# Constant matmuls ahead of weight blocks, earlier value loads, a mask moved to TensorE, and paired reciprocals

## The chip, the cores and the metric

The kernel runs on one core of a Trainium2 chip. The metric is the device time of one execution in microseconds (us). TensorE does the matmuls and transposes, VectorE and ScalarE the element-wise work, GpSimd a share of the latter, and SyncE (SP) issues every transfer between memory and the core's buffer. Each engine works through its own instructions in the order in which they were written; semaphores tie the engines together.

## The reference, cut to what matters

Three layers in a row, all in fp32: attention with a causal mask and a bias from cumulated sums, a gated layer without an activation, and a layer with a squared ReLU.

```python
# q, k, v: (4, 8, 576, 64), s: (4, 8, 576); q and k are eight times 0.1 * randn
cum    = np.cumsum(np.maximum(s, 0.0), axis=-1)
bias   = -(cum[..., :, None] - cum[..., None, :])
scores = 0.125 * q @ k^T + np.minimum(bias, 0.0)      # -1e9 above the diagonal
attn   = softmax(scores);   x = (attn @ v), as (2304, 512)
x      = ((x @ w_a) * (x @ w_b)) @ w_out              # 512 -> 1536 -> 512
out    = np.maximum(x @ w_in, 0.0) ** 2 @ w_out2      # 512 -> 2048 -> 512
```

## The kernel before, in words

The order of all instructions is written by a planner (class `Plan`). The kernel first traces every operation with the engines that may run it, an estimated cost for each, and the buffers that it takes. `Plan.order` then simulates the engines with these costs: at each step it takes, for the engine that is free first, the most urgent operation that is ready. Urgency is the stream ("first", "next", "att", "moe", "late", "fill") and then the order of tracing. A transfer may be issued while no more than 3 us of planned transfers are outstanding; a buffer of a tag is handed out in the order of tracing. An operation may carry a `lag`, a time to add to its readiness. A changed cost or lag can thus change the order everywhere behind it.

`Plan.run` emits the instructions in that order. An operation on TensorE may carry a number `idle`: so many matmuls of a constant tile `warm` (128 x 512, bf16) are emitted just ahead of it, into the PSUM bank that the operation itself writes (`op.bank`). The planner sets `idle` by itself where it sees a gap of over 400 ns ahead of an operation, and takes the larger of that and a number that was set by hand; by hand it is set to 6 ahead of the first scores of heads 0 and 2. The constants take no time in the plan. They stop where the pools are swapped, after the attention.

Attention works on a batch at a time, two heads (a pair) at a time, the queries cut into blocks of 96 and four times 120 rows. `softmax` makes a head's scores in PSUM, in five diagonal pieces (the last block has one more, without the diagonal): in the first batch (`b == 0`) by fp32 matmuls of `fq` and `fk`, whose 65th row holds the cumulated sums; in the others by two fp32r matmuls of split operands. The causal mask has two forms, by the constant `MASKED`. For `b < MASKED` a further matmul adds a triangle of -1e9 (`mask`, bf16, times the identity `plain`) to the diagonal's columns, and VectorE reduces the scores to the negated maximum (`neg`). Otherwise one VectorE operation, recorded as CUSTOM_DVE_ANT_0 and followed by a read of its accumulator, adds the mask, negates the scores in PSUM and gives the minimum; the exponential then takes a scale of -1. ScalarE's exponential (`e<-st,neg`) leaves row sums in `tot`; VectorE adds them into `one` and takes the reciprocal of a head's five columns. `weigh` transposes the weights (`pt`), copies them (`ph`) and multiplies them with the values (`av`); `divide` multiplies the pair's result with the reciprocals of both heads.

The sums start the kernel: `ssb` is loaded, VectorE scans it into `cum`, and a row of `cum` per head is sent by a transfer to the 65th row of `fk`. The values of the very first pair carry a lag of `SUMS_FIRST` = 5800 ns. The tag of the value tiles has two buffers.

Then comes `moe1`, the gated layer, in chunks of 512 tokens. A block `fstep(f)`, f from 0 to 11, makes two half blocks in banks of the tag "mm", which has three buffers: `ab{c}_{f}_0` with `w_a` and `ab{c}_{f}_1` with `w_b`, twelve matmuls each. ScalarE copies the first to `a`, VectorE multiplies the second with it in its bank, ScalarE and VectorE then split the product from that bank into `gh` and `gl`. Three blocks are summed with `w_out` (`py`). Chunk 0 uses the first batch's tokens while the weights are still being decoded: `split_w(f)` loads the three pieces of 512 KB of a block, a few raw buffers at a time (`roomxh`, `roomxl`, `words`), and VectorE, ScalarE and GpSimd turn them into `wh` and `wl`. Interleaved with chunk 0 runs the attention of the second batch. Later chunks load what chunk 0 stored. The squared-ReLU layer follows after the swap.

All instructions of the program are recorded under line 261 (constants: 256), so tiles tell them apart.

Of the kernel before, what the change touches and what calls it, by code (L numbers as in the profile page):

```python
# [16 lines left out]
P = 128  # L17
# [246 lines left out]
def attention_moe_moe(tc, q, k, v, s, w_a, w_b, w_out, w_in2, w_out2, out):  # L264
# [28 lines left out]
    SOON = 2  # L293
    BEHIND = 2
    AHEAD = 5
    SUMS_FIRST = 5800.0
    LATE_DOWN = 7
    APART = 2
    READY = 6
# [1 line left out]
    pl = Plan(nc)  # L301
# [55 lines left out]
    def dve(*args, reads=(), **kw):  # L357
        pl.call(on_dve(*args, **kw), reads=reads)
# [53 lines left out]
    def load_values(b, p):  # L412

        t = at([P, NJ, P], F32, "val", 2, f"val{b}_{p}")
        j = 0
        while j < len(kb):
            k0, m = kb[j]
            j1 = j + 1
            while j1 < len(kb) and kb[j1][1] == m:
                j1 += 1  # L420
            dma(
                t[:m, j:j1].part(j),
                v[b, p, k0 : k0 + m * (j1 - j)].rearrange("(j t) c -> t j c", t=m), m * (j1 - j) * 0.5,
                lag=SUMS_FIRST if b == 0 and p == 0 else 0.0,
            )
            for i in range(j, j1):
                values[b, p, i] = t[:m, i].part(j)
            j = j1
# [66 lines left out]


    HALF = S // 2
    MASKED = 1
    banks = [[(2, 0, 336), (0, 0, 96)], [(1, 0, 216), (LAST, 0, HALF)], [(LAST, HALF, HALF)], [(3, 0, 456)]]
    places = {0: ("e0", 432, 0), 2: ("e0", 432, 96), 1: ("e1", 672, 0), 3: ("e1", 672, 216), LAST: ("e2", S, 0)}  # L500

# [84 lines left out]
    def softmax(b, p, h, head, one):  # L586

        nq = len(kb)
        nm = f"{b}_{p}_{h}"
        hh = 2 * p + h  # L590
        neg, tot = small[count[1] % 4]
        count[1] += 1
        tiles, place, held = {}, {}, []
        for blk, (tag, width, off) in places.items():
            if tag not in tiles:
                tiles[tag] = at([P, width], F32, tag, 3, f"{tag}{nm}")
            place[blk] = (tiles[tag], off)
        for i, pieces in enumerate(banks):
            ps = mm_bank(f"st{nm}_{i}") if b == 0 and i % 4 > 1 else bank(f"st{nm}_{i}")
            off = 0  # L600
            calls, cost, got = [], 0, []
            for blk, k0, kn in pieces:
                at_, m = kb[blk]
                qc = slice(at_, at_ + m)
                to = ps[:m, off : off + kn]
                diag = at_ >= k0 and at_ + m <= k0 + kn
                ks = slice(k0, k0 + kn)
                if b == 0:
                    tq, tk = head
                    both = ((tq[: D + 1, qc], tk[: D + 1, ks]),)  # L610
                    cost += 4 * kn / 2.4 + 13
                else:
                    t1, t2q, t2k = head
                    both = ((t1[:66, 0, qc], t1[:66, 1, ks]), (t2q[:, qc], t2k[:, ks]))
                    cost += 2 * (kn / 2.4 + 15)
                calls += [("matmul", (to, *ab), {"stop": True}) for ab in both]
                if diag and b < MASKED:
                    tri = mask[:m, EDGE : EDGE + m]
                    calls.append(("matmul", (to[:, kn - m :], plain[:m, :m], tri), {"stop": True}))
                    cost += 70  # L620
                e, eo = place[blk]
                got.append((blk, k0, m, to, kn, diag, e[:m, eo + k0 : eo + k0 + kn]))
                off += kn
            if b == 0:
                ins = [tq.part("x"), tq.part("c"), tk.part("x"), tk.part("c")]
            else:
                ins = [t1, t2q, t2k]
            if b < MASKED:
                ins += [plain, mask]

            for z, (_, _, kw) in enumerate(calls):
                kw.update(start=z == 0, skip_group_check=z > 0)
            pe(cost, calls, ps, ins)
            if b == 0 and i == 0 and hh in (0, 2):
                pl.ops[-1].idle = 6
            for blk, k0, m, to, kn, diag, _ in got:
                c = blk if k0 == 0 else nq
                if not diag or b < MASKED:
                    dve("tensor_reduce", kn, out=neg[:m, c : c + 1].part(c), in_=to, op=ALU.max, axis=AX.X, negate=True)
                    continue  # L640
                edge = EDGE + m
                dve(
                    "tensor_tensor_reduce", kn + 135, out=to, in0=to, in1=mask[:m, edge - kn : edge], op0=ALU.add,
                    op1=ALU.min, scale=-1.0, scalar=3.0e38, accum_out=neg[:m, c : c + 1].part(c),
                )
            held += got
            whole = [x for x in held if x[0] != LAST or pieces[0][0] == LAST]
            held = [x for x in held if x not in whole]
            if pieces[0][0] == LAST:
                dve(  # L650
                    "tensor_reduce", 2, out=neg[:, nq + 1 : nq + 2].part(nq + 1), in_=neg[:, nq - 1 : nq + 1],
                    op=ALU.min, axis=AX.X, reads=[neg.part(nq - 1), neg.part(nq)],
                )
            for blk, k0, m, to, kn, diag, ee in whole:
                c = blk if k0 == 0 else nq
                n_ = nq + 1 if blk == LAST else blk
                act(
                    "activation", kn + 360, ee.part((blk, k0)), to, AF.Exp, bias=neg[:m, n_ : n_ + 1].part(n_), scale=-1.0 if diag and b >= MASKED else 1.0,
                    accum_out=tot[:m, blk, int(c == nq) : int(c == nq) + 1].part(c), psum=True,
                )  # L660
        qs = one[:, h * nq : h * nq + nq].part(h)
        dve(
            "tensor_reduce", 3 * nq, out=qs, in_=tot[:, :nq], op=ALU.add, axis=AX.X,
            reads=[tot.part(c) for c in range(nq + 1)],
        )
        dve("reciprocal", nq * 6, qs, qs)
        return place

    def weigh(b, p, places, chunk, u):
# [58 lines left out]
    def divide_far(b, p, one, u):  # L728

        nq = len(kb)  # L730
        ps = bank(f"rs{b}_{p}", "t")
        pe(107, [("transpose", (ps[: 2 * nq, :P], one, ident), {})], ps, [one.part(0), one.part(1), ident])
        rows = at([P, P], F32, "rows", 2, f"rows{b}_{p}")[: 2 * nq]
        copy(P, rows, ps[: 2 * nq, :P], psum=True)
        far = rd[b, p]
        dma(far, rows, 2)
        wide = at([P, nq * P], F32, "wide", 2, f"wide{b}_{p}")[:, :S]
        for h in range(2):
            to, f0 = wide[h * D : h * D + D], h * nq
            dma(to[:, :HEAD].part((h, 0)), far[f0 : f0 + 1, :HEAD].to_broadcast([D, HEAD]), 24)  # L740
            dma(
                to[:, HEAD:].rearrange("p (j q) -> p j q", q=BODY).part((h, 1)),
                far[f0 + 1 : f0 + nq, :BODY].rearrange("(o j) q -> o j q", o=1).to_broadcast([D, LAST, BODY]), 123,
            )
        kw = {"out": u, "in0": u, "in1": wide, "op": ALU.mult}
        pl.call(on_gps("tensor_tensor", S, **kw), on_dve("tensor_tensor", S, two=True, **kw))
# [29 lines left out]
    def attention(b):  # L776
        steps = []

        def unit(p):
            st = {}  # L780
# [4 lines left out]
            def one(h):  # L785
                def f():
                    if h == 0:
                        st["u"] = at([P, S], F32, "u", 2, f"u{b}_{p}")
                        st["one"] = at([P, 2 * len(kb)], F32, "one", 2, f"one{b}_{p}")
                    st[h] = softmax(b, p, h, st["h"][h], st["one"])  # L790
                    if h == 1:
                        u = st["u"]
                        for chunk in weight_banks:
                            weigh(b, p, (st[0], st[1]), chunk, u)
                        divide(b, p, st["one"], u)
                        if b == 0:
                            xh, xl = first_x(p, 0, FIRST)
                            copy(FIRST, xh, u[:, :FIRST])
                            subtract(FIRST, xl, u[:, :FIRST], xh.bitcast(F32))
                            dma(xd[b][0][p].part(p), u[:, FIRST:], (S - FIRST) * 0.5)  # L800
                        else:
                            dma(xd[b][0][p].part(p), u, S * 0.5)

                return f
# [203 lines left out]
    def moe1(c):  # L1008
# [16 lines left out]
        def fstep(f):  # L1025
            def g():
# [9 lines left out]
                for i in range(2):  # L1036
                    ps = mm_bank(f"ab{nm}_{i}")[:, :n]
                    pairs = []
                    for d in range(ND):
                        xh, xl = st["x"](d, 0, n)  # L1040
                        li = lo[i][:, d, :] if first_chunk else lo[:, i, d, :]
                        pairs += [(wh[f, i][:, d, :], xh), (wh[f, i][:, d, :], xl), (li, xh)]
                    matmul(ps, n, pairs)
                    pp.append(ps)
                a_sb = sb([P, 512], F32, "a", 2, f"a{nm}")[:, :n]
                act("copy", n, a_sb, pp[0], psum=True)
# [549 lines left out]
```

## Time and profile before

| | |
|---|---|
| time, median of 3 runs (lowest, highest) | 1039.75 us (1036.43, 1042.04) |
| the profiled execution's own time; its span | 1038.9 us; 1037.1 us |
| TensorE busy | 1006.6 us, 97% of the span |
| VectorE busy | 749.8 us, 72% |
| ScalarE busy | 611.6 us, 59% |
| GpSimd busy | 332.8 us, 32% |
| mean granted TensorE clock | 0.993 |
| transfers, mean | 235 GB/s |

The span runs from the first to the last instruction of the profiled execution. Recorded ends of matmuls are modelled and overlap, so the distance from one start to the next tells what a matmul takes of the engine. In a timeline a row holds instructions of one kind merged: start, length until the last one ends, engine, line, operation, `out<-in`, partitions and shape, count, and in brackets the idle time ahead of it with what ended it. The mean clock of a stretch lies between 0.5 and 1.0, as parts of it were granted 1.2 GHz or 2.4 GHz.

### The profile page before, as it was taken

The numbers are of one execution on the slowest core, as the hardware profiler recorded it, in microseconds if no ns is written. First come the engines' busy times: TensorE is split into PE (matmuls) and PEld (weight loads), VectorE is DVE, ScalarE is ACT, GpSimd is POOL, SyncE is SP. The second block draws the span as 40 slices with busy tenths as digits, with TensorE's granted clock in tenths as the row PEclk, the third lists the DMA queues.
The fourth block names the chain that finished last, engine by engine and source line by source line (L and its number), as shares of the span: only waits on it lengthen the run. The fifth ranks groups of instructions, "written<-read, shape, count | busy, mean of one in ns | idle before, by whom it ended". The sixth has DMA issues, their size and how long they took to land.

```text
span 1037.1 us, 16855 instructions
## 1 busy us (share of the span) xinstructions
PE 1006.6 (97%) x5634; PEld 871.1 (84%) x5641; DVE 749.8 (72%) x1556; ACT 611.6 (59%) x1385; POOL 332.8 (32%) x299
## 2 busy tenths in 40 slices
PE   8999999998999999999989999999999999999998
PEld 4668776766777777788879899989999999999998
DVE  6888777857677757555677888778777666876566
ACT  6786776756676655343333544577556665657562
POOL 3225553425343534211232223212225212441123
PEclk9999999998999999999999999999999999999999
DMA  8447688687887776757655767599978967778764
GB/s 252 143 130 214 217 255 263 202 265 204 228 239 223 216 228 208 237 175 236 214 192 141 256 189 257 174 305 370 342 246 304 316 234 258 264 256 288 256 235 162
DMA packets 139255, 243.55 MB, mean 235 GB/s; under 512 B 21273, under 2 KB 91025, under 8 KB 139169
## 3 DMA queue, kind: packets, MB, share of 16 engines
q1 hardware_dynamic: 139168, 242.49, 72.0%
q8 instruction: 44, 0.72, 0.3%
q14 instruction: 43, 0.34, 0.1%
HBM read 181.46 MB, written 52.11 MB: 225 GB/s over the span
## 4 chain that ended last, share of the span: by engine, by line
PE 73%; DMA 10%; DVE 5%; issue 2%; ACT 2%; SPq 1%; POOL 0%; DVEq 0%; ACTq 0%; POOLq 0%
PE ab L261 14%; PE pa L261 8%; PE py L261 7%; PE po_0t L261 6%; PE pc L261 4%; PE pw L261 4%; PE wa L261 4%; PE av L261 3%; PE pt L261 3%; PE st L261 2%; PE wc L261 2%; PE pb L261 2%; PE po_3b L261 2%; PE po_2b L261 2%; PE po_1b L261 2%
## 5 line engine op out<-in xcount | busy, mean ns | idle before, releaser
L261 ACT ACTIVATE e<-st,neg 120x216 f32<-120x216 f32 (+2 forms) x192 | 93.2, 490 | 26.9 <-DVE neg L261 23.6
L261 PE MATMUL py<-g,wh 128*128 128x512 f32 x288 | 91.5, 399 | 0.7 <-DVE y L261 0.7
L261 PE MATMUL ab<-xh,wh 128*128 128x512 f32 x192 | 76.3, 398 | 0.0
L261 PE MATMUL ab<-xh,lo 128*128 128x512 f32 x192 | 75.0, 391 | 0.0
L261 PE MATMUL ab<-xl,wh 128*128 128x512 f32 x192 | 74.9, 390 | 0.0
L261 PE MATMUL pt<-ident,e 120*120 120x120 f32 (+2 forms) x480 | 69.6, 272 | 2.9 <-ACT e L261 1.6
L261 PEld LDWEIGHTS pt<-ident,e 120*120 120x120 f32 (+2 forms) x480 | 50.7, 135 | 21.8 <-issue 8.9
L261 PE MATMUL ab<-x,wh 128*128 128x512 f32 x192 | 62.3, 406 | 2.6 <-ACT a L261 2.6
L261 PE MATMUL av<-ph,val 120*64 120x240 f32 (+3 forms) x512 | 60.5, 366 | 1.1 <-DVE ph L261 1.1
L261 PEld LDWEIGHTS py<-g,wh 128*128 128x128 f32 x288 | 52.0, 188 | 10.7 <-DVE y L261 1.0
L261 DVE CUSTOM_DVE_ANT_0 st<-st,mask 96x96 f32<-96x96 f32 (+4 forms) x120 | 52.8, 455 | 8.5 <-PE st L261 6.0
L261 PE MATMUL py<-g,loo 128*128 128x512 f32 x144 | 56.6, 393 | 0.6 <-DMA loo<-wlo 0.6
L261 DVE TENSOR_TENSOR ab<-ab,a 128x512 f32<-128x512 f32 x36 | 25.1, 698 | 40.2 <-PE ab L261 40.2
L261 PEld LDWEIGHTS av<-ph,val 120*64 120x64 f32 (+1 forms) x512 | 31.9, 138 | 26.3 <-issue 13.8
L261 DVE COPY ph<-pt 120x360 f32<-120x360 f32 (+3 forms) x79 | 40.5, 524 | 14.2 <-PE pt L261 13.8
L261 ACT COPY ph<-pt 96x336 f32<-96x336 f32 (+3 forms) x81 | 35.3, 449 | 25.9 <-PE pt L261 25.2
L261 PE MATMUL st<-T 66*120 66x336 f32 (+1 forms) x144 | 45.2, 329 | 3.8 <-ACT e L261 3.8
L261 PEld LDWEIGHTS ab<-x,wh 128*128 128x128 f32 x192 | 35.6, 192 | 10.2 <-ACT a L261 2.7
L261 PEld LDWEIGHTS ab<-xh,lo 128*128 128x128 f32 x192 | 36.1, 188 | 7.8
L261 PEld LDWEIGHTS ab<-xh,wh 128*128 128x128 f32 x192 | 36.1, 188 | 7.1 <-issue 0.4
L261 PEld LDWEIGHTS ab<-xl,wh 128*128 128x128 f32 x192 | 36.1, 188 | 6.7
L261 ACT CAST g<-ab 128x512 fp32r<-128x512 f32 x36 | 21.0, 582 | 33.4 <-DVE ab L261 33.4
(692 smaller groups left out, 3160.2 us busy)
## 6 DMA issues: line engine op xcount, KB each, us to landing
w<-w2q SPq DMA_DIRECT2D x48, 896.0 KB
lo<-wlab SPq DMA_DIRECT2D x36, 512.0 KB
w2q<-w2ip SPq DMA_DIRECT2D x48, 256.0 KB
w2s<-w2op SPq DMA_DIRECT2D x48, 256.0 KB
loo<-wlo SPq DMA_DIRECT2D x24, 384.0 KB
w2ir<-in_moe_w_in SPq DMA_DIRECT2D x16, 512.0 KB
w2or<-in_moe_w_out SPq DMA_DIRECT2D x16, 512.0 KB
ws_0t<-w2s SPq DMA_DIRECT2D x12, 512.0 KB
```

The source lines that it names most:

```text
L261: getattr(eng, method)(*map(real, args), **{k: real(a) for k, a in kw.items()})
```

## The change

Four edits. The values of the first pair are loaded without a lag. The softmax of the second batch (`b == 1`) takes the masking by matmuls, as the first batch does. The reciprocal is taken once for a pair, over the ten columns of both heads, after the second head's sums, in place of once a head over five. In chunk 0, from the fourth block on, `idle` is set to 3 for the first half block and to 1 for the second.

```diff
-    SUMS_FIRST = 5800.0
+    AHEAD_AB = (3, 1)
...
                 v[b, p, k0 : k0 + m * (j1 - j)].rearrange("(j t) c -> t j c", t=m), m * (j1 - j) * 0.5,
-                lag=SUMS_FIRST if b == 0 and p == 0 else 0.0,
             )
...
-    MASKED = 1
+    MASKED = 2
...
             reads=[tot.part(c) for c in range(nq + 1)],
         )
-        dve("reciprocal", nq * 6, qs, qs)
         return place
...
-        pe(107, [("transpose", (ps[: 2 * nq, :P], one, ident), {})], ps, [one.part(0), one.part(1), ident])
+        pe(107, [("transpose", (ps[: 2 * nq, :P], one, ident), {})], ps, [one, ident])
...
                     if h == 1:
-                        u = st["u"]
+                        u, sums = st["u"], st["one"]
+                        dve("reciprocal", len(kb) * 12, sums, sums)
                         for chunk in weight_banks:
...
                     matmul(ps, n, pairs)
+                    if first_chunk and f >= 3:
+                        pl.ops[-1].idle = AHEAD_AB[i]
                     pp.append(ps)
```

## Rows read from the trace of the kernel before

**Rows 1.** The page, part 1: busy us, share of the span, instructions.
```profile
PE 1006.6 (97%) x5634; PEld 871.1 (84%) x5641; DVE 749.8 (72%) x1556; ACT 611.6 (59%) x1385; POOL 332.8 (32%) x299
```

**Rows 2.** Stages: length; busy PE, PEld, DVE, ACT, POOL; clock; DMA share; GB/s.
```profile
0.00:13.29 13.29, 10.59 (x36) 4.13 (x37) 6.09 (x9) 6.34 (x10) 3.15 (x26) 1.00 0.68 205
...
24.96:77.63 52.67, 52.10 (x372) 35.11 (x375) 43.83 (x117) 41.20 (x115) 14.15 (x11) 1.00 0.46 138
77.63:182.76 105.13, 101.03 (x520) 79.03 (x520) 84.27 (x191) 75.15 (x171) 49.93 (x35) 0.98 0.77 237
182.76:251.91 69.15, 65.07 (x382) 47.74 (x383) 50.49 (x136) 46.35 (x125) 28.61 (x22) 0.95 0.76 230
```

**Rows 3.** TensorE's waits, 104.8 to 214: us in total, times, longest us.
```profile
PE ab L261 <- ACT a L261: 2.6, 1, 2.6
PE pt L261 <- ACT e L261: 1.1, 1, 1.1
```

**Rows 4.** TensorE's waits, 214 to 251.9.
```profile
PE st L261 <- ACT e L261: 2.5, 3, 1.2
```

**Rows 5.** Two stretches in the columns of rows 2: where the clock falls.
```profile
169.00:182.00 13.00, 10.42 (x42) 8.37 (x41) 9.30 (x18) 9.33 (x21) 3.72 (x3) 0.87 0.98 302
...
234.00:247.00 13.00, 10.35 (x51) 6.96 (x52) 9.51 (x30) 8.15 (x22) 9.13 (x7) 0.74 0.91 256
```

**Rows 6.** Timeline of the first 14 us: the scan and SP's transfers.
```profile
3.42 1.34 DVE L261 TENSOR_TENSOR_SCAN cum<-spos 32x576 f32<-32x576 f32 x1
...
3.70 0.59 SPq L261 DMA_DIRECT2D roomxh<-in_moe_w_a  x1
...
5.50 1.22 SPq L261 DMA_DIRECT2D fk<-cum  x2
...
7.86 5.33 SPq L261 DMA_DIRECT2D val<-in_v  x4
```

**Rows 7.** The same timeline: ScalarE scales the second head's query.
```profile
7.85 0.68 ACT L261 ACTIVATE fq<-fq 64x576 f32<-64x576 f32 x1 [1.49 <-DMA fq<-in_q]
```

**Rows 8.** TensorE's timeline from 13 to 30 us.
```profile
13.29 0.80 PE L261 MATMUL st<-fk,fq 65*120 65x336 f32 x2 [1.25 <-DMA fk<-cum]
13.92 0.22 PE L261 MATMUL st<-mask,plain 120*120 120x120 bf16 x1
13.98 0.36 PE L261 MATMUL st<-fk,fq 65*96 65x96 f32 x2
...
20.45 0.59 PE L261 MATMUL glow<-warm 128*128 128x512 bf16 x2
...
21.48 0.81 PE L261 MATMUL glow<-warm 128*128 128x512 bf16 x3
...
23.25 1.46 PE L256 MATMUL st<-warm 128*128 128x512 bf16 x6
24.96 0.83 PE L261 MATMUL st<-fk,fq 65*120 65x336 f32 x2 [0.25 <-DVE fq L261]
```

**Rows 9.** TensorE's timeline: a half block of chunk 0.
```profile
178.05 1.22 PE L261 MATMUL ab<-x,wh 128*128 128x512 f32 x2 [2.58 <-ACT a L261]
```

**Rows 10.** Timelines of VectorE and ScalarE, 163 to 184 us.
```profile
171.92 0.70 DVE L261 TENSOR_TENSOR ab<-ab,a 128x512 f32<-128x512 f32 x1 [2.48 <-PE ab L261]
...
181.23 0.68 DVE L261 TENSOR_TENSOR g<-ab,g 128x512 fp32r<-128x512 f32 x1
...
177.42 0.57 ACT L261 COPY a<-ab 128x512 f32<-128x512 f32 x1
```

**Rows 11.** VectorE's groups by shape: count, busy us, mean ns, idle before, releaser.
```profile
L261 DVE CUSTOM_DVE_ANT_0 st<-st,mask 120x456 f32<-120x456 f32 x24 | 15.2, 635 | 4.9 <-PE st L261 3.8 <-ACT ph L261 0.3 <-ACT e L261 0.3
L261 DVE DVE_READ_ACCUMULATOR2_ANT neg<- 120x1 f32 x96 | 13.4, 139 | 0.0
L261 DVE RECIPROCAL one<-one 128x5 f32<-128x5 f32 x32 | 5.8, 183 | 0.4
L261 DVE TENSOR_REDUCE neg<-st 120x1 f32<-120x456 f32 x8 | 5.0, 623 | 0.1
```

## The prediction

> **What bounds the kernel now.** I read the page first: TensorE is busy 1006.6 of the span's 1037.1 us, VectorE 749.8 [rows 1]. Only 30 us of the span are not TensorE's, so an edit pays through TensorE alone: it removes matmul time, fills a wait, or keeps the clock up. The stage table comes next, because this change touches only the first 252 us [rows 2]. The reader is to see there that 2.7 of the first 13.29 us are idle and most of the "busy" rest is constant matmuls; that 52.10 of the 52.67 us of the first batch's attention from 24.96 on are busy; and that the first chunk (77.63 to 182.76) is busy 101.03 of 105.13. These stages are bound by TensorE, with small holes.
>
> Then I looked for the holes. From 104.8 to 214 TensorE's waits are one of 2.6 us, one of 1.1, and two of 0.2 that are not shown [rows 3]; from 214 to 251.9 the largest sum is 2.5 us in three waits for exponentials [rows 4]. The granted clock is at its full level except in two places here: a mean of 0.87 over 169:182 and 0.74 over 234:247 [rows 5]. With two levels, 1.00 and 0.50, that is 3.4 and 6.8 us at 1.2 GHz, and half of it is lost: 1.7 and 3.4 us. The first low stretch follows the 2.58 us wait at 178.05 [rows 9].
>
> **The change, part by part.** The sum is made against the profiled execution: 1038.9 us, which is 1.8 above its span and 0.85 below the median of 1039.75. Half a per cent, 5.2 us, is about what a measurement of this kernel can tell.
>
> *First values at once.* SP issues in this order now: loads of the first heads, three weight pieces of 512 KB from 3.70 on, the two rows of sums at 5.50, two small stores, and four loads of values from 7.86 on, one after the other until 13.19 [rows 6]. TensorE's first real matmul stands at 13.29, released by the row of sums [rows 8], 7.8 us after that row was issued: its bytes queue behind the weights. Without the lag the values are ready at time zero and belong to the most urgent stream, so they take the slots from 3.70. The second pair's tile may be taken as soon as the first's is, so its 48 KB load goes along. When these are out the sums are ready (the scan ends at 4.76 [rows 6]), so the sums' rows go out near their old time, and the weights come behind them. Ahead of the sums stand then the last first-head load, which lands at 7.85 (the wait of the scaling for it ends there [rows 7]), and 48 + 240 + 48 = 336 KB of values; at the 205 GB/s of the stage [rows 2] 1.6 us. So the first real matmul at about 9.5 in place of 13.29: 3.8 us. Bounds: 5.4 if the values cost nothing (7.85), 1.3 if one weight piece (2.5 us at that rate) still goes ahead.
>
> The second gap, 20.4 to 24.96, is held by constants and 0.25 us of wait for the second pair's first query [rows 8]; 11 constants at 0.216 are 2.4 us. That load comes behind weight pieces too and can close by 0 to 2.6 us; I take 0, since the weights move later into its way.
>
> The cost: the first weight piece goes from 3.70 to about 8.3, behind some eight issues of 0.6, and the decode behind it on VectorE and ScalarE loses the idle time before 13.29. Its cover is the stage to 77.63, where VectorE works 43.83 and ScalarE 41.20 of 52.67 us and the DMA engines are 0.46 busy [rows 2]. If the cover fails, the first chunk waits up to 4.6 us for weights. I take cover.
>
> *Constants ahead of the blocks.* Blocks four to twelve, two halves each, 3 + 1 constants: 36. A run of six of them took 1.46 us with 0.38 the last [rows 8], so 0.216 each and 7.8 us in all. The Trainium skill (TensorE: Matmul & The Clock Gate, Back-to-back issue gap) gives about 216 ns for the isolated case and 131 for a sustained stream at 512 columns; by the latter they would be 4.7 us and the sum 3.1 lower. The row agrees with the isolated figure.
>
> They cost nothing only where TensorE would wait anyway, and it waits ahead of just one of these 18 halves, at 178.05 [rows 3, 9]. That wait ends with ScalarE's copy at 177.42, 0.57 long [rows 10]. The other two banks were still to be read by VectorE at 181.23 and after [rows 10], so it is the bank that is awaited; and the constants write that same bank. They can't start before the wait ends. So in line on a busy engine: 7.8 us gross. Against it stands that a later TensorE meets later waits shorter: weights and exponentials go on meanwhile. What can be absorbed is 1.1 + 0.2 + 0.2 + 2.6 = 4.1 us of wait [rows 3] and, if the low clock goes with the wait, 1.7. The chain into the long wait passes VectorE work that itself waited 2.5 us for the half block before [rows 10], so part of it moves along with TensorE. I take the 4.1 and half of the 1.7: net 2.9 us, bounds 2.0 and 7.8.
>
> The skill's page named above (What's actually happening) has the throttle follow how busy the array was lately; by that rule constants ahead of a block would spare the 1.7 us at 178. The rows show that low stretch behind a wait that these constants can't fill; no row shows them inside one.
>
> *Second batch masked by matmuls.* 8 heads with 5 diagonal blocks: 40 more matmuls of at most 120 columns. In the first batch such a matmul starts at 13.92 and the next at 13.98 [rows 8]: 0.06 us, 2.4 in all on TensorE. (Bounds: 0, if in waits, and 40 of the recorded 0.22 us, 8.8, which overlap their neighbours; the start times decide.) VectorE trades a custom operation for a reduction: 635 against 623 ns on the longest block [rows 11]; at 12 ns each that is under 1 us over 40. The custom form is followed by a read of its accumulator, 139 ns each [rows 11], 5.6 us at most, and hardly visible, since the next operation starts with it (181.23 in [rows 10]). VectorE is not the bound: 84.27 of 105.13 us [rows 2]. Zero, with the bound that all of it shortens waits for exponentials.
>
> *One reciprocal a pair.* 16 reciprocals of 183 ns fewer [rows 11], 2.9 us of VectorE in the whole kernel, hidden by TensorE. The first head's waits for the second's; only the division of the pair reads it. Zero; at most those 2.9.
>
> Sum: -3.8 + 2.9 + 2.4 = +1.5 us: 1040.4 against 1038.9. The written order also changes everywhere, since the planner's costs for the second batch and start do; that moves waits after 252 us either way. I forecast **1040**.
>
> **The rivals.**
> *The start pays twice and the softmax waits go (faster).* The second gap closes too: -3.8 - 2.6. The lighter VectorE chain of the second batch spares the 2.5 us of waits around 230 to 238 and the low clock behind them, 3.4 [rows 4, 5]. With +2.4 and +2.9 that is -7.0: 1032. For it: these waits end on exponentials, which wait for maxima on VectorE. Against: the reduction is no shorter than the custom operation.
>
> *The constants stay in line (slower).* Place: the 18 half blocks. Price: all 7.8 instead of 2.9. With -3.8 and +2.4 that is +6.4: 1045. It decides from an absorption under 1.2 us on. For it: 17 halves without a wait. Against: the waits of 1.1 and 2.6 are fed by transfers and decoding that would go on.
>
> *The weights come late (slower).* TensorE reaches the first block 3.8 us earlier and waits there for weights issued 4.6 us later: the gain at the start turns into +4.6, the constants hide in these waits (0), the masks stay: +7.0, 1046. For it: ScalarE, 41.20 of 52.67 us, runs decode in program order. Against: the slack named above.
>
> *No change at all at the start:* if the planner puts the weights ahead of the sums' rows after all, the 3.8 shrinks to 1.3 and the sum is +4.0: 1043, still within half a per cent.
>
> **How the numbers follow.** Within half a per cent 0.40 (forecast 0.33, start unchanged 0.07); faster 0.34 (the start paying twice 0.24, and 0.10 for a new order that spares waits: some 19 us of TensorE's idle time lie behind 252 us, its 30.5 less what [rows 2] leave idle); slower 0.26 (constants in line 0.16, weights late 0.10). The likeliest one's own range is 1036 to 1044. For 8 in 10 the range takes in the rivals at 1032 and 1046 with the spread of a new order, about 5 us, beyond either: 1027 to 1051.
>
> **What would show each step.** Start: the first real matmul near 9.5 us, the values issued from 3.70, the first weight piece after the sums' rows; wrong if a weight load still precedes them. Cover: the first block near 73.8; wrong if it stays at 77.6. Constants: 36 rows between blocks four and twelve with 0.216 from start to start and no idle ahead; the span from first block to the end of the chunk longer by 2 to 8 us. If instead they stand where the half block waits for weights, they are free. Masks: 40 more rows of 0.06 spacing before 252 us. Clock: a full level at 169 to 182 speaks for absorption. Most of all the prediction would be wrong if the new order, not the four edits, sets the waits: then stages after 252 us differ by more than those before it.

## The result and the profile after

The changed kernel takes 1042.98 us (median of 10 runs, 1039.93 to 1046.25), the kernel before 1036.22 in 10 runs on the same chips. The ratio is 1.0068, 95% interval 1.0048 to 1.0089: about 7 us slower. The time lies inside the forecast range of 1027 to 1051 and 3 us above the forecast of 1040; the likeliest case, no change beyond half a per cent, did not come. The two profiled executions differ by less, 1042.4 against 1038.9 us, because that of the kernel before is 2.7 us slower than its median.

The page of the changed kernel, part 1, against [rows 1]: busy time and instructions of each engine.
```profile
PE 1014.3 (97%) x5717; PEld 877.8 (84%) x5717; DVE 752.0 (72%) x1502; ACT 609.5 (59%) x1383; POOL 331.4 (32%) x299
```
TensorE has 7.7 us more work in a span that is 3.5 us longer (1040.6). VectorE has no less, though 40 custom operations became reductions.

The first microseconds, from the timeline of all engines, against [rows 6, 8], and below them two rows of TensorE's timeline:
```profile
3.71 1.57 SPq L261 DMA_DIRECT2D val<-in_v  x3
...
5.40 1.23 SPq L261 DMA_DIRECT2D fk<-cum  x2
...
8.31 0.42 SPq L261 DMA_DIRECT2D roomxh<-in_moe_w_a  x1
...
10.08 0.73 PE L261 MATMUL st<-fk,fq 65*120 65x336 f32 x2
```
```profile
20.05 1.46 PE L256 MATMUL st<-warm 128*128 128x512 bf16 x6
21.35 0.73 PE L261 MATMUL st<-fk,fq 65*120 65x336 f32 x2
```
Values, sums' rows, weights: the order that the prediction read out of the code, and the first weight piece at 8.31 as it said. The first real matmul comes at 10.08 and no longer waits for the sums' row but stands behind its own six constants; the next pair's begin at 21.35 in place of 24.96. Two executions tell the size of this gain only roughly. In the nine profiles of this case with the lag on the values the first real matmul stands at 11.75 to 13.29, and the kernel before is the latest of them; in four of the nine (e1, e8, e9, e11) it does not wait for the sums' row either. In the five without the lag it stands at 8.64 to 10.08.

The stage table of the changed kernel (columns as in [rows 2]): start, rest of the first batch's attention, first chunk from the first to the last of its half blocks, and from there to the first block of the next chunk.
```profile
0.00:10.08 10.08, 8.63 (x27) 3.47 (x28) 3.27 (x4) 3.98 (x6) 3.15 (x26) 1.00 0.55 143
21.35:74.40 53.05, 52.05 (x373) 34.91 (x372) 41.77 (x109) 40.39 (x116) 17.64 (x14) 1.00 0.45 125
74.40:226.30 151.90, 149.44 (x830) 115.15 (x829) 115.27 (x237) 104.08 (x247) 71.03 (x51) 0.99 0.76 228
226.30:255.80 29.50, 26.75 (x159) 18.61 (x157) 19.50 (x48) 17.77 (x50) 6.00 (x5) 0.94 0.82 246
```
The kernel before, cut at the same events, and in its third row the wide chunk further on (first matmul of `wa` to that of `pa`):
```profile
77.60:211.80 134.20, 130.10 (x686) 101.85 (x686) 107.74 (x248) 97.58 (x228) 62.91 (x44) 0.99 0.75 230
211.80:251.90 40.10, 36.02 (x216) 24.94 (x217) 27.03 (x77) 23.94 (x68) 15.62 (x13) 0.91 0.82 249
520.10:666.30 146.20, 141.17 (x772) 130.92 (x772) 117.28 (x203) 63.63 (x113) 40.78 (x41) 0.99 0.65 207
```
The first half block starts 3.2 us earlier (74.4 against 77.6), and the next chunk 3.9 us later (255.8 against 251.9). Between the two lie 181.4 us in place of 174.3. The work between them is arranged anew (more of the second batch's attention stands before the last half block), so only the sum of the two stages compares. TensorE's idle time in them fell from 8.2 to 5.2 us: what grew is its work. Stages of single executions differ by some us without any change: from the next chunk's first block to the end, with one and the same order of work, the kernel before takes 785.2 us here, and e1, e2 and e5 below 781.4, 777.7 and 780.1.

Two of the constants' rows in TensorE's timeline of the changed kernel:
```profile
98.49 0.81 PE L256 MATMUL ab<-warm 128*128 128x512 bf16 x3
...
138.38 3.40 PE L256 MATMUL ab<-warm 128*128 128x512 bf16 x15
```
Not one of the rows that hold these constants shows idle time ahead of it. Ahead of the half block at 138.38 the planner itself saw a gap in its new order and set 15, and 2 ahead of one more; so 32 of the 36 are the edit's own.

### The profile page after: what moved, and what is told of

Read it like the earlier page. It is cut to its first block, busy times and chain, and to the rows that moved or that the text cites. A ratio compares the mean times of both kernels' runs of the same rounds, so it can differ in the third digit from the quotient of the medians.

```text
span 1040.6 us, 16980 instructions
## 1 busy us (share of the span) xinstructions
PE 1014.3 (97%) x5717; PEld 877.8 (84%) x5717; DVE 752.0 (72%) x1502; ACT 609.5 (59%) x1383; POOL 331.4 (32%) x299
## 4 chain that ended last, share of the span: by engine, by line
PE 74%; DMA 9%; DVE 5%; ACT 2%; SPq 1%; issue 1%; POOL 0%; DVEq 0%; ACTq 0%; POOLq 0%
PE ab L261 15%; PE pa L261 8%; PE py L261 7%; PE po_0t L261 6%; PE pc L261 4%; PE pw L261 4%; PE wa L261 4%; PE st L261 3%; PE av L261 2%; PE pt L261 2%; PE wc L261 2%; PE pb L261 2%; PE po_3b L261 2%; PE po_2b L261 2%; PE po_1b L261 2%; PE po_0b L261 2%
## 5 line engine op out<-in xcount | busy, mean ns | idle before, releaser
L261 PE MATMUL ab<-x,wh 128*128 128x512 f32 x192 | 65.1, 420 | 0.0
L261 DVE TENSOR_REDUCE neg<-st 120x1 f32<-120x288 f32 (+3 forms) x112 | 46.6, 442 | 24.1 <-PE st L261 15.1
L261 ACT COPY ph<-pt 120x360 f32<-120x360 f32 (+3 forms) x79 | 34.4, 445 | 22.0 <-PE pt L261 19.9
L261 PE MATMUL st<-t2k,t2q 128*120 128x336 f32 (+1 forms) x144 | 40.7, 301 | 1.5 <-POOL t2k L261 1.5
```

The costliest lines, as they stand in the source:

```text
L261: getattr(eng, method)(*map(real, args), **{k: real(a) for k, a in kw.items()})
```

## The experiments

Where it says "same order", the lists of instructions of all engines differ from those of the kernel it is held against in nothing but the operations named. Ratios are to the kernel before, which ran beside them (median 1034.7 to 1034.8); 0.1% is 1.03 us. The ratios stand as they were recorded, with their intervals; quotients of the medians differ from them by up to 0.2% (0.9939 for e9, 1.0126 for e12), within the intervals.

| run | constants | values | masks | one reciprocal | median us | ratio (95%) |
|---|---|---|---|---|---|---|
| e1 | yes | | | | 1038.70 | 1.0049 (1.0013 to 1.0085) |
| e2 | double | | | | 1046.07 | 1.0117 (1.0078 to 1.0156) |
| e3 | | yes | | | 1032.56 | 0.9988 (0.9963 to 1.0013) |
| e4 | | yes | yes | yes | 1036.41 | 1.0022 (0.9998 to 1.0045) |
| e5 | | | in the order of before | | 1037.03 | 1.0012 (0.9986 to 1.0038) |
| e6 | | | order only | | 1025.20 | 0.9916 (0.9885 to 0.9947) |
| e7 | | | yes | | 1026.82 | 0.9924 (0.9897 to 0.9950) |
| e8 | | | | yes | 1034.46 | 0.9995 (0.9965 to 1.0025) |
| e9 | yes | | yes | | 1028.47 | 0.9922 (0.9895 to 0.9950) |
| e10 | | yes | yes | | 1032.54 | 0.9982 (0.9953 to 1.0012) |
| e11 | | | yes | yes | 1036.50 | 1.0012 (0.9982 to 1.0041) |
| e12 | | yes | | yes | 1047.78 | 1.0107 (1.0061 to 1.0154) |

### The constants, in three orders: e1, e2, e4, e9

e1 adds to the kernel before, and e2 with (6, 2):
```diff
+    AHEAD_AB = (3, 1)
...
                     matmul(ps, n, pairs)
+                    if first_chunk and f >= 3:
+                        pl.ops[-1].idle = AHEAD_AB[i]
```


> The kernel before with the 36 constants alone; the planned order stays that of before. Theory A (they stand in line on a busy TensorE): 7.8 us gross, little absorbed, 6 to 8 us slower than before. Theory B (waits behind them take them up, as the prediction summed): 2 to 4 us slower. Theory C (the new order of the other edits made the loss, the constants cost nothing): within 1 us of before.

> The kernel before with 6 and 2 constants ahead of the half blocks, 72 in all, order as before. Theory A: twice the loss of the single dose, 12 to 16 us. Theory B: the waits are used up by the first 36, so the second 36 cost their full 7.8 us: 10 to 12 us. Theory C: within 2 us of before.

The first chunk in e1, and in e2 (stage tables):
```profile
76.50:216.40 139.90, 137.61 (x722) 106.24 (x721) 106.06 (x248) 98.06 (x228) 61.67 (x44) 0.99 0.72 222
```
```profile
77.20:224.40 147.20, 144.97 (x758) 109.81 (x757) 104.91 (x248) 98.38 (x228) 61.69 (x44) 0.99 0.68 210
```
134.2 became 139.9 and 147.2: in these profiles the first 36 constants, 7.8 us at 0.216, cost 5.7, the second 36 cost 7.3. Idle time went from 4.1 to 2.3 and stayed there. Whole runs agree: +5.1 us (1.3 to 8.8) and +12.1 (8.1 to 16.1). Their middle values lie between theories A and B for the single dose and where the two meet for the double one; the intervals are too wide to tell A from B, but theory C is out. What is left of the waits is this, in e1's timeline of TensorE, against [rows 9]:
```profile
180.65 0.38 PE L256 MATMUL ab<-warm 128*128 128x512 bf16 x1 [2.23 <-ACT a L261]
```
It is now the constant that waits for ScalarE's copy, since it writes the same bank as the half block behind it; then the half block follows. The wait moved along with TensorE and lost 0.35 of its 2.58 us. The low clock behind it stayed too, as a 13 us stretch of e1 around it shows against the first of [rows 5]:
```profile
174.00:187.00 13.00, 10.77 (x45) 8.64 (x45) 10.11 (x26) 8.37 (x22) 4.33 (x3) 0.87 0.98 313
```

e4 is the changed kernel without the four lines of the constants, same order.

> The changed kernel without the constants; its planned order is that of the changed kernel. Theory A: 6 to 8 us faster than the changed kernel, so between 1 us faster and 1 slower than before. Theory B: 2 to 4 us faster than the changed kernel, 3 to 5 slower than before. Theory C: like the changed kernel, 6 to 7 us slower than before.

1.0022 against the changed kernel's 1.0068: the 32 constants cost about 4.8 us in this order also (0.46%, each ratio with 0.2% to either side, so some 1.5 to 8 us). By the middle values the constants make most of the loss, and theory C fails here. The first chunk of e4, against 151.90 with 149.44 busy:
```profile
74.90:224.50 149.60, 145.71 (x798) 112.44 (x797) 117.18 (x237) 103.71 (x247) 71.47 (x51) 0.98 0.76 232
```
Of its 2.3 us of difference not all is the constants': ahead of the place of the first of them e4 lost more to the low clock (a mean of 0.75 from 85.0 to 98.4, 0.87 in the changed kernel). From that place to the next chunk the changed kernel takes 157.3 us (98.49 to 255.80) and e4 153.6 (100.15 to 253.70): 3.8 us, of 6.9 that 32 constants come to.

> The mask edit and the 36 constants, in the order of the masks alone. Theory A and B: the constants cost as in the two other orders, 4 to 7 us, so 2 to 5 us faster than before in all. Theory C (what the constants cost depends on the order): under 2 us or over 9.

In the third order, that of the masks alone, they cost nothing that can be told: 0.9922 against 0.9924 for e7 (0.3% to either side each). That is theory C's lower case, but the two intervals together leave room for a cost of up to some 4 us, and the medians alone would give 1.6. The first chunk of e6 (this order, with neither masks nor constants), its waits for exponentials, and the same two views of e9:
```profile
77.20:217.40 140.20, 133.79 (x708) 104.64 (x707) 116.82 (x267) 101.72 (x244) 58.97 (x42) 0.99 0.76 232
```
```profile
PE st L262 <- ACT e L262: 4.5, 3, 2.2
```
```profile
76.10:219.80 143.70, 141.33 (x776) 110.70 (x783) 113.55 (x227) 102.01 (x244) 59.40 (x42) 1.00 0.74 228
```
```profile
PE st L261 <- ACT e L261: 0.6, 1, 0.6
```
6.4 us idle became 2.4: this order has waits for exponentials that a later TensorE finds shorter (4.5 to 0.6), and 36 constants with 40 masks, 10.2 us at 0.216 and 0.06 each, lengthen the chunk by 3.5 us only. A low clock of e6 (a mean of 0.66 from 150 to 155) is gone as well. In these two profiles, then, what a matmul in line costs depends on the waits that the order holds behind it.

### The values alone: e3

```diff
                 v[b, p, k0 : k0 + m * (j1 - j)].rearrange("(j t) c -> t j c", t=m), m * (j1 - j) * 0.5,
-                lag=SUMS_FIRST if b == 0 and p == 0 else 0.0,
```


> The kernel before with the values at once alone. Theory A and B: the first real matmul at about 10.1 us as in the changed kernel, and the gain of 3.2 us at the first block stays: 2 to 4 us faster. Theory D (weights come late): the first block early, but the first chunk's end where it was or later: 0 to 5 us slower.

1.2 us faster, from 3.8 faster to 1.3 slower. The first chunk, the way to the next one, and the wide chunk:
```profile
75.20:215.50 140.30, 131.19 (x680) 102.43 (x679) 112.50 (x255) 98.51 (x234) 63.87 (x46) 0.98 0.77 231
215.50:254.90 39.40, 35.10 (x228) 24.42 (x226) 29.20 (x79) 25.32 (x70) 21.70 (x19) 1.00 0.92 264
521.70:663.10 141.40, 139.14 (x775) 130.26 (x775) 117.04 (x205) 63.63 (x115) 41.58 (x37) 1.00 0.66 215
```
The first half block is 2.4 us early (75.2), the next chunk 3.0 us late (254.9; in e5, with the order of before, the two stand at 76.3 and 252.2): the gain is spent in the first chunk, where 9.1 us are idle in place of 4.1. TensorE's waits up to 262 us in e3, then ScalarE's waits in the first chunk of e3:
```profile
PE st L261 <- ACT e L261: 8.5, 6, 2.7
```
```profile
ACT roomxh L261 <- DMA roomxh<-in_moe_w_b: 9.8, 4, 3.9
ACT e L261 <- DVE neg L261: 6.9, 5, 3.2
```
From TensorE's timeline, and below it three links of the chain of work:
```profile
141.53 0.59 PE L261 MATMUL st<-T 66*120 66x288 f32 x1 [2.68 <-ACT e L261]
```
```profile
140.85 6.06 DMA roomxh<-in_moe_w_b
146.93 0.69 ACT roomxh L261
147.64 0.43 DVE roomxl L261
```
The chain of work runs through loads of weights of 6 us each (another starts at 178.84): ScalarE stands at the decode of a piece that has not landed (9.8 us in four waits), VectorE behind it, and the maxima and exponentials of the second batch are queued behind both. That fits theory D up to the next chunk, but it does not show that late weights are the cause. ScalarE's waits for weight pieces in the first chunk add up to 15.6 us in e3 (9.8 + 2.2 + 3.6) and to 12.2 before. The piece that is issued at 140.85 went out at 129.92 before; in e4, which has the early values too, it goes out at 142.12, and TensorE is idle for only 3.9 us in the first chunk there. e3 has an order of its own and was not run in that of before, so late weights and new order are not separated.

Why the whole run is not slower is open. From 254.9 to the end e3 takes 776.0 us, against 785.2 from 251.9 before, but 777.7 to 781.4 in e1, e2 and e5 with the order of before; between 2 and 9 us come back there, part of it in the wide chunk (141.4 us against 143.4 to 147.2 in these four).

### The masks, operations and order apart: e5, e6, e7

The planner traces one form and the program emits another; e5 plans the form of before and emits the masks, e6 the reverse.
```diff
-            for method, args, kw in op.ways[op.eng][1]:
+            for method, args, kw in op.alt or op.ways[op.eng][1]:
...
-    MASKED = 1
+    MASKED = 1      # e6: 2; what the planner sees
+    EMITTED = 2     # e6: 1; what is emitted (scores' matmuls, VectorE's reduction, sign of the exponential)
```


> Order of every engine as before; the 40 masks of the second batch are emitted as matmuls and plain reductions in the places of the custom operations. Theory A (the masks lie in line on TensorE): 2 to 3 us slower than before. Theory E (VectorE's shorter chain pays more than the masks cost): 1 to 3 us faster. Theory F (only the new order of the masked batch matters): within 1 us of before.

> The order that the planner writes with the masks, but the custom operations emitted as before and no mask matmul in the second batch. Theory A: within 1.5 us of before. Theory F: the whole effect of the mask edit stands here, 2 us or more to either side.

> The mask edit alone, with its own order. Theory A: 2 to 3 us slower than before, and 2 to 3 slower than the same order without masks. Theory E: faster than that order without masks. Theory F: like it within 1 us.

In the order of before the masks cost 1.2 us (1.4 faster to 3.9 slower). Their place in TensorE's timeline of e5:
```profile
102.13 0.22 PE L262 MATMUL st<-mask,plain 120*120 120x120 bf16 x1
102.16 0.38 PE L262 MATMUL st<-T 66*120 66x288 f32 x1
```
In their own order they cost 0.8 us (0.9924 against 0.9916). The direction is theory A's, the size below it, and neither is clear of noise. The order without them is 8.7 us faster than before (5.5 to 11.9): theory F. To an order belong the constants that the planner sets at the gaps it sees: the trace of e5 has 89 weight loads of `warm`, that of e6 81, and eight at 0.216 are 1.7 us at most, an estimate. The mask edit alone makes the kernel faster, and not through its operations. One place of the gain, the wide chunk: the stage in e6, then TensorE's wait for its second bank before and in the changed kernel:
```profile
514.00:655.50 141.50, 139.10 (x775) 130.22 (x775) 117.64 (x205) 63.67 (x115) 41.74 (x37) 1.00 0.67 215
```
```profile
PE wb L261 <- DVE y L261: 2.4, 1, 2.4
```
```profile
PE wb L261 <- DVE y L261: 2.2, 1, 2.2
```
Before, VectorE's work ahead of the result that frees this bank stood 2.42 us in wait for a load:
```profile
536.09 2.08 DVE L261 TENSOR_TENSOR ws<-wh,lo 128x512 f32<-128x512 f32 x2 [2.42 <-DMA lo<-wlab]
```
Behind that wait the clock is low again, in the kernel before as in the changed one; a stretch of before around it:
```profile
535.00:548.00 13.00, 10.60 (x49) 9.71 (x48) 7.79 (x15) 2.99 (x6) 2.02 (x2) 0.87 0.68 228
```
The stage takes 146.2 us with the wait, 146.4 in the changed kernel, 143.4 to 147.2 in e1, e2, e4 and e5, which have a wait of 1.0 to 2.2 us there, and 141.4 to 142.6 where the profile has none of it (e3, e6 to e12). In e6 the rest of its gain is spread over the other stages, and its causes stay open.

### The reciprocal and the pairs: e8, e10, e11, e12

e8 takes out `dve("reciprocal", nq * 6, qs, qs)` and adds, ahead of the weighing, `dve("reciprocal", len(kb) * 12, sums, sums)`; the others combine the edits of the table.

> The paired reciprocal alone, with its own order. As predicted: within 1.5 us of before, since VectorE is not the bound. Theory F widened (any new order moves the waits): 2 us or more to either side, although only 16 short operations go.

> Values at once and masks, no constants, reciprocals a head. If effects add up (theory G): 1 + 8 = 9 us faster than before. Theory F (each order sets its own waits): the sum fails by 3 us or more; if the late weights of the values edit are what spoils the masked order, 1 us faster to 3 slower, as for the three edits together.

> Masks and paired reciprocals, values with their lag. Theory G: 8 us faster than before. Theory F: off that sum by 3 us or more.

> Values at once and paired reciprocals, masks as before. Theory G: 1.5 us faster than before. Theory F: off that sum by 3 us or more to either side. In all orders without the 2.2 us wait of the wide chunk's second bank for VectorE, the stage from its first matmul to the next layer should take 141 to 142 us, with it 144 to 147.

Alone the reciprocal is worth nothing that can be told (0.5 us faster, 3.6 faster to 2.6 slower). The sums of the single effects fail three times: values and masks 0.18% faster where 0.88 was the sum, masks and reciprocal 0.12% slower where 0.81 faster was the sum, values and reciprocal 1.07% slower where 0.17 faster was the sum. Theory G falls. e12's largest wait is a single one, a half block that waits for the bank that VectorE is to free:
```profile
PE ab L261 <- DVE g L261: 6.3, 1, 6.3
```
For these three the order was not separated from the operations as in e5 and e6; that their effect is one of order is argued from the size of the edits, not shown.

e6 and e7, with 1025.2 and 1026.8 us, beat both kernels.

## Why the prediction was right or wrong

**The number.** The forecast added 1.5 us to a base of 1038.9; measured were 6.8 us on top of 1036.2. That 1040 came within 3 us of 1042.98 is in part luck: the base was 2.7 us too high, the sum 5.3 us too low.

**What bounds the kernel** held: the loss is TensorE's work, and in the two profiles it lies ahead of 256 us; behind it the changed kernel takes 784.8 us and the kernel before 785.2. As the order of before also came out at 777.7 to 781.4 there (e1, e2, e5), a few us of loss behind are not excluded.

**Values at once.** The order of the transfers, the first weight piece at 8.3 and the first block near 73.8 (74.4) came as forecast; the real start is 3.2 us early, predicted 3.8. The 13.29 that the term started from was itself the latest of nine; by the means of the profiles with and without the lag (12.2 and 9.4) the gain is 2.9. What failed is "I take cover". The stage to the first block does cover the later decoding, but the first chunk of e3 does not keep the gain: TensorE is idle for 9.1 us there in place of 4.1, and the gain is gone by the next chunk. The rival "the weights come late" put its price at the first block; the waits that came stand 65 us behind it, at exponentials, and whether late weights or the new order make them is not separated. As a term the start is worth 1.2 us by e3, from 3.8 faster to 1.3 slower, so the predicted 3.8 lies at the edge.

**Constants ahead of the blocks.** The gross price of 7.8 us and the reason, that they can't run inside the wait for a bank that they write themselves, are shown by e1 and e2. The net term was set too low by the middle values: 2.9 us against 5.1 (e1) and 4.8 (changed kernel against e4), within the bounds of 2.0 to 7.8. The intervals of these two (1.3 to 8.8, some 1.5 to 8) do not exclude 2.9; the trace of e1 shows the step that failed. It is "I take the 4.1 and half of the 1.7": in e1 1.8 us of waits were absorbed and no low clock went. The 2.6 us wait counted there moved along, as the sentence on the chain said it might. The rival "the constants stay in line" is the one nearest to what happened; with 1045 it went too far by the 2 to 3 us that were absorbed.

**Masks.** 2.4 us predicted, 1.2 and 0.8 measured in two orders; the intervals hold both 0 and 2.4. That VectorE gains nothing held: reductions of the longest block take 627 ns in the changed kernel, and in e5, with the order held, nothing is faster for it.

**Reciprocals.** Zero predicted, none that can be told measured.

**The written order** got no term in the sum, only a chance of 0.10 and some 5 us of spread. It is the largest effect found: 8.7 us for the order of the masks alone, which is shown, and 7 to 13 us between the sums of single edits and their combinations, where it is argued. That the changed kernel shows none of the gain of the masks' order is the luck of this combination: e4, all edits but the constants, is 0.22% slower, while its parts one by one would make 0.93% faster. The test that the prediction set, that stages behind 252 us would differ more than those ahead, did not come true for the changed kernel (0.4 us behind, 3.9 ahead). It asks more than one profile can tell: the part behind differs by 7.5 us between four profiles of one order.

## What to carry to other kernels

Where a planner writes the order, run an edit twice: once in the old order, with only the emitted operation changed, and once in the new order with the old operation; else the effect of the operation (1 us here) can't be told from that of the order (9 us). Constant matmuls ahead of a wait for the bank that they write, or in a stage without waits, cost nearly their full 0.216 us each (7.3 of 7.8 us for the second dose of e2); that they are free where the bank is free and an input is late follows from this, but no run here shows it. Compare stages of two profiles only after a look at how far profiles of one order lie apart. An earlier start can be spent in the next stage: ask which transfers were put off for it, and which in-order engine stands at them later.

## What was not expected of the hardware

In the order of before the clock did not follow the constants. In the kernel before, in e1 and in e2 a 13 us stretch around the same half block has a mean clock of 0.87, although 27 and 54 constants were run in the blocks before it in e1 and e2. In e2 the stretch from 224.4 to 264.5, behind the first chunk, had a mean clock of 0.87, lower than the 0.91 of the kernel before there. In the order of the masks it was otherwise: e6 has a mean of 0.66 from 150 to 155, e9, with the constants and shorter waits, 1.00 over the whole first chunk. One profile of each shows it.

A reciprocal of ten columns takes 210 ns in the changed kernel, against 183 of five [rows 11]: the fixed part is most of it.
